# Score products of an attention layer on four quarters of the array, in a kernel on one Trainium2 core

## The chip, the cores and the metric

The kernel is one program on one core of a Trainium2 chip. The metric is the device time of one execution in microseconds, as the median of several runs. A profiled execution of the kernel before was traced instruction by instruction; all rows below come from that trace.

## The reference

Four batches of 768 positions go through windowed attention with attention sinks (8 heads of 64), and then through a channel MLP with a low-rank mixing term over positions. Everything is fp32.

```python
scores = q @ k^T / sqrt(64)                    # B=4, H=8, S=768, D=64
keep = (key < n_sink) | (0 <= query - key < window)   # n_sink=4, window=128
a = softmax(where(keep, scores, -1e9)); attn = a @ v  # (B, H, S, D)
x = attn.transpose(0, 2, 1, 3).reshape(B, S, 512)
u = x + ((x^T @ U) @ V)^T                      # U: 768x32, V: 32x768
out = u + relu(u @ w_ch1) @ w_ch2              # 512 -> 2048 -> 512
```

So each query sees at most 128 keys of its window, which ends at the query itself, and four sinks.

## The kernel before, in words

Queries are cut into six blocks of 128 per head, and heads are worked in four pairs per batch: in `qp` and `kp` the head dimension of one head lies on partitions 0 to 63 and that of the other on 64 to 127. Keys are laid out block by block, each block as four sink columns followed by its 128 keys. The scores of a query block are therefore one product with 260 neighbouring columns: the previous block's 128 keys, the four sinks, the own block's 128 keys. The first query block has no previous one and takes 132.

`scores` (the function printed below) emits, for one query block and both heads of the pair, one step on TensorE: two fp32 calls of 64 rows x 128 columns of weights (the queries) with 260 or 132 moving columns, each into its own PSUM bank. After it, for each head: VectorE copies, under the predicate `past` (key after query), the scores of the previous block over those of the own block (L734), so that 132 columns are left per query, adds the mask and takes the row's extreme (L736), and ScalarE takes the exponent with the row sum (L739). `normalise` scales the rows (L749, L757, L760), `transposes` turns three blocks (L777) and splits them into an own part and a previous part (L783, L787), and `values` multiplies with the values (L812): there the two heads lie in two column halves of the array, 128 rows x 64 columns each.

The attention of batch 0 stands at the start of the program. That of batch 1 is spread over the feed-forward products of batch 0 (L1032 to L1034 and L1054), and those of batches 2 and 3 over the products of batch 1 (L1198). Batches 1 to 3 form their feed-forward layers with fewer products over sums of quarter matrices; their weights come by DMA from DRAM (`w<-wd`, `w<-ws`) and the sums go through VectorE (L1203).

Nothing runs in the order in which it is written. Each function adds steps to a `Plan`, with a price in us, the buffers that it reads and writes, and a priority; `Plan.order` simulates all engines, tries 41 orders and keeps the one with the lowest cost by its prices. PSUM has eight banks, and a step takes whichever is free first. A step on TensorE is marked `tiled` when it runs on parts of the array, and the plan charges 0.2 us (`SWITCH`) for each change between tiled and whole and prefers to put tiled steps together. `after=self.gate` keeps the score steps of later batches from starting before a given feed-forward step.

Of the kernel before, what the change touches and what calls it, by code (L numbers as in the profile page):

```python
# [21 lines left out]
P = 128  # L22
B, H, S, D = 4, 8, 768, 64
# [65 lines left out]
def f32(ap):  # L89
    return ap.bitcast(F32)  # L90
# [185 lines left out]
class Plan:  # L276
# [7 lines left out]
    def add(self, eng, dur, fn, *args, port=False, **kw):  # L284
        return self.any({eng: (dur, fn, port)}, *args, **kw)
# [235 lines left out]
def dve(n):  # L521
    return 0.069 + n * 1.042e-3
# [6 lines left out]
def act(n):  # L529
    return 0.052 + n * 0.8333e-3  # L530
# [6 lines left out]
class Fast:  # L537
# [19 lines left out]
    def fixed(self, n, shape, dtype, name):  # L557

        ring = Ring(n, None)

        def get(view=lambda t: t):
            return ring(lambda i=len(ring.boxes) % n: view(self.place(name, i, shape, dtype)))
        get.ring, get.name = ring, name
        return get
# [146 lines left out]
    def scores(self, blocks, t0, q, k, rows):  # L711
        nc, add = self.nc, self.plan.add
        (qr, qbase), (kr, kbase) = q, k
        todo = []
        for qb in blocks:
            half, u = divmod(qb, NBLK)
            if half not in rows:
                rows[half] = self.p(), self.mn(), self.sm()
            lo = P if qb == 0 else 0
            k0 = max(qb - 1, 0) * SW + (NS if qb else 0) - kbase  # L720
            for i in range(2):
                todo.append((i, qb, u, lo, UW - lo, qb * P - qbase, k0, self.bank(), rows[half]))

        def mms():
            for i, _, _, _, wd, q0, k0, st, _ in todo:
                at = slice(i * D, (i + 1) * D)
                nc.tensor.matmul(st()[:, :wd], qr()[at, q0:q0 + P], kr()[at, k0:k0 + wd], start=True, stop=True)  # L727
        add("PE", 0.005 + sum(max(x[4], 131) for x in todo) / 1200.0, mms, r=[qr, kr] + [(x[8][0], (x[0], x[2])) for x in todo],
            w=[x[7] for x in todo], prio=t0, after=self.gate, tiled=True)
        for i, qb, u, lo, wd, _, _, st, (p, mn, sm) in todo:  # L730
            row = lambda p=p, i=i, u=u: p()[:, i, u]
            at = lambda t, i=i, u=u: t()[:, i * NBLK + u:i * NBLK + u + 1]
            if qb:
                add("DVE", dve(P), lambda st=st: nc.vector.copy_predicated(st()[:, SW:UW], self.past, st()[:, :P]),  # L734
                    w=(st,), prio=t0)
            add("DVE", dve(SW), lambda st=st, row=row, at=at, wd=wd, qb=qb, mn=mn: nc.vector.tensor_tensor_reduce(  # L736
                row(), st()[:, wd - SW:wd], self.mask[:, min(qb, 2)], -0.125, 3.0e38, ALU.add, ALU.min, at(mn)),
                r=(st,), w=((p, (i, u)), (mn, (i, u))), prio=t0)
            add("ACT", act(SW) + 0.22, lambda row=row, at=at, mn=mn, sm=sm: nc.scalar.activation(  # L739
                row(), row(), AF.Exp, bias=at(mn), scale=-1.0, accum_out=at(sm)),  # L740
                r=((mn, (i, u)),), w=((p, (i, u)), (sm, (i, u))), prio=t0)
# [50 lines left out]
    def values(self, parts, t0, v, xT):  # L792
        nc, add = self.nc, self.plan.add
        vr, kb0 = v
        todo, cost, outs = [], 0.0, []
        for half, tops in parts:
            pa = self.bank()
            kbs = range(max(half * NBLK - 1, 0), (half + 1) * NBLK)
            for n, kb in enumerate(kbs):
                lo = 2 * (kb - half * NBLK) + 1  # L800
                hi = min(lo + 2, 2 * NBLK)
                lo = max(lo, 0)
                at = max(kb - half * NBLK, 0) * P
                for i, t in enumerate(tops):
                    todo.append((pa, i, t, kb - kb0, lo * P, hi * P, at, n == 0, n == len(kbs) - 1))
            cost += 1.09 if half == 0 else 1.31
            outs.append((half, pa))

        def run():
            for pa, i, t, kb, lo, hi, at, first, last in todo:  # L810
                mv = t().rearrange("p u s j -> p (u s j)")[:, lo:hi]
                nc.tensor.matmul(pa()[i * D:(i + 1) * D, at:at + hi - lo], vr()[:, i, kb, :], mv,  # L812
                                 start=first, stop=last, skip_group_check=True)
        add("PE", cost, run, r=[vr] + [t for _, tops in parts for t in tops] + [(xT, half) for half, _ in parts],
            w=[pa for _, pa in outs], prio=t0, tiled=True)
        for half, pa in outs:
            self.copy(CH, lambda half=half: xT()[:, half * CH:(half + 1) * CH], lambda pa=pa: pa()[:, :CH], psum=True,
                      r=(pa,), w=((xT, half),), prio=t0)
# [127 lines left out]
    def sink_mix(self, half, rep, t0):  # L946

        nc, add = self.nc, self.plan.add
        vsr, by, tp, _, _, reps = self.late
        reps.append(rep)  # L950
        if half == 0:
            return

        def run():
            for blk in range(NB):
                nc.tensor.matmul(by()[:, :P], reps[blk // NBLK]()[:, blk % NBLK * P:(blk % NBLK + 1) * P],
                                 self.usf()[:, blk, :], start=blk == 0, stop=blk == NB - 1)
        add("PE", 1.32, run, r=reps + [self.usf, self.T[0]], w=(by,), prio=t0)
        part = self.pst(lambda t: f32(t)[:, :P])
        add("DVE", dve(P), lambda: nc.vector.tensor_scalar(part(), by()[:, :P], 0.25, None, ALU.mult),  # L960
            r=(by,), w=(part,), prio=t0)
        add("PE", mm(DM, 4), lambda: nc.tensor.matmul(
            tp(), part(), vsr().rearrange("p n d -> p (n d)"), start=False, stop=False),
            r=(part, vsr), w=(tp,), prio=t0)

    def warm(self, tp, t0):

        nc, bank, rows = self.nc, self.bank(), self.mask.rearrange("p a b -> p (a b)")

        def run():  # L970
            for _ in range(NWARM):
                nc.tensor.matmul(bank()[:, :3 * SW], self.ident, rows, start=True, stop=True)
        return self.plan.add("PE", mm(3 * SW, 4 * NWARM), run, r=(tp,), w=(bank,), prio=t0)
# [365 lines left out]
    def run(self):  # L1339
        tc, nc, ctx, ring, one, fixed = self.tc, self.nc, self.ctx, self.ring, self.one, self.fixed  # L1340
# [10 lines left out]
        self.ust, self.vst = fixed(1, [P, NB, P], F32R, "ust")(), fixed(1, [P, S], F32R, "vst")()  # L1351
        self.t = fixed(2, [P, DM], F32R, "t")
        self.wtiles, self.banks, self.bigs, self.accs = [], [], list(self.early), []
        bigs = Ring(NBIG, None)
        self.raw, self.end = self.share(bigs, self.bigs, lambda t: t), self.share(bigs, self.bigs, lambda t: f32(t[:, :DM]))
        self.rest = None
# [48 lines left out]
        for b in range(B):  # L1405
            prio = 70.0 + 80.0 * NCHUNK * b
# [296 lines left out]
```

## Time and profile before

| | |
|---|---|
| median of 3 runs | 680.77 us (680.75 to 680.93) |
| span of the profiled execution | 680.2 us |
| TensorE matmul busy | 665.4 us, 98% |
| VectorE busy | 532.9 us, 78% |
| ScalarE busy | 438.7 us, 64% |
| GpSimd busy | 256.1 us, 38% |

The span goes from the first to the last instruction of the profiled execution; the runs are timed apart from it. The time that lies around the span is not in the trace, and the median of the runs is 0.57 us above it. TensorE's busy time is a sum of overlapping records whose ends are modelled, so the starts of its records tell more than their durations.

### The profile page before, as it was taken

Reading aid. Unit: us, or ns where it says so; the run is one execution under the profiler, and the core shown is the slowest. Engines: PE = TensorE matmul, PEld = TensorE weight load, DVE = VectorE, ACT = ScalarE, POOL = GpSimd, SP = SyncE. Lnnn points to the kernel's source line nnn. Section 1 sums busy time; section 2 is a strip of 40 time slices with the busy share of each in tenths; the row PEclk is TensorE's granted clock in tenths of the full one; section 3 lists DMA queues with packets and bytes.
Section 4 is the critical chain, followed back from the end, with each engine's and each line's share of the span. In section 5 each row is a group of like instructions: output and inputs, shape, how many; then the busy total and the mean of one; then the engine's idle time right before and its main releaser. Section 6 shows DMA issues by size and latency. Waiting matters only on the chain.

```text
span 680.2 us, 12939 instructions
## 1 busy us (share of the span) xinstructions
PE 665.4 (98%) x3990; PEld 595.0 (87%) x3990; DVE 532.9 (78%) x1498; ACT 438.7 (64%) x1197; POOL 256.1 (38%) x310
## 2 busy tenths in 40 slices
PE   7998999999999999999999999999999999999996
PEld 5666888788889888888898799999999999999996
DVE  7989999999998888889788799655735974673483
ACT  6997698889665378885788786355436535543551
POOL 3742545547535244576473361202303311020120
PEclk9999999999999999999999999999999999999999
DMA  8649999988869699996999856899788899988883
GB/s 288 202 154 368 374 320 353 365 286 309 295 253 336 234 340 357 324 341 191 317 336 306 272 180 189 266 359 306 243 259 252 248 311 331 298 246 259 248 267 104
DMA packets 135982, 191.94 MB, mean 282 GB/s; under 512 B 10336, under 2 KB 106208, under 8 KB 135904
## 3 DMA queue, kind: packets, MB, share of 16 engines
q1 hardware_dynamic: 135616, 190.63, 83.9%
q8 instruction: 34, 0.56, 0.3%
q10 hardware_dynamic: 288, 0.39, 0.2%
q14 instruction: 44, 0.36, 0.2%
HBM read 141.70 MB, written 49.28 MB: 281 GB/s over the span
## 4 chain that ended last, share of the span: by engine, by line
PE 83%; DVE 10%; DMA 3%; ACT 2%; issue 1%; POOL 1%; SPq 0%; ACTq 0%; DVEq 0%
PE bank L1198 48%; PE bank L1054 10%; PE bank L727 5%; PE bank L812 4%; PE bank L1032 3%; PE bank L1033 3%; PE bank L1034 3%; PE bank L777 2%; DVE p L736 1%; PE bank L919 1%; DMA kp<-ud 1%; DMA w<-wd 1%; DVE w L608 1%; DVE bank L734 1%; DVE oph L783 1%
## 5 line engine op out<-in xcount | busy, mean ns | idle before, releaser
L1198 PE MATMUL bank<-w,w 128*128 128x384 f32 x678 | 133.1, 339 | 0.1
L1198 PEld LDWEIGHTS bank<-w,w 128*128 128x128 f32 x678 | 118.2, 188 | 4.4 <-issue 1.9
L739 ACT ACTIVATE p<-p,mn 128x132 f32<-128x132 f32 x192 | 75.9, 398 | 9.5 <-DVE mn L736 9.1
L1198 PE MATMUL bank<-w,spare 128*128 128x384 f32 x342 | 65.1, 335 | 0.0
L1203 DVE TENSOR_TENSOR big<-bank,big 128x384 f32<-128x384 f32 x84 | 44.7, 553 | 24.6 <-PE bank L1198 24.0
L610 POOL TENSOR_TENSOR w<-uh,w 128x384 fp32r<-128x384 f32 x22 | 23.2, 1054 | 105.7 <-ACT w L601 102.6
L1054 PE MATMUL bank<-w,hh 128*128 128x512 f32 x192 | 61.9, 404 | 0.0
L1198 PEld LDWEIGHTS bank<-w,spare 128*128 128x128 f32 x342 | 60.0, 188 | 0.0
L610 POOL TENSOR_TENSOR spare<-spare 128x128 f32<-128x128 f32 (+1 forms) x56 | 39.2, 705 | 43.0 <-DVE spare L608 17.8
L727 PE MATMUL bank<-kp,qp 64*128 64x260 f32 (+1 forms) x360 | 52.9, 392 | 1.1 <-DMA qp<-in_q_dram 0.4
L736 DVE CUSTOM_DVE_ANT_0 p<-bank,mask 128x132 f32<-128x132 f32 x192 | 50.6, 287 | 0.1
L1032 PE MATMUL bank<-ul,w 128*128 128x384 f32 x128 | 44.4, 347 | 0.9 <-POOL ul L610 0.6
L727 PEld LDWEIGHTS bank<-kp,qp 64*128 64x128 f32 x360 | 31.1, 186 | 16.0 <-issue 4.8
L734 DVE COPY_PREDICATED bank<-past,bank 128x128 f32<-128x128 int32 x160 | 41.5, 289 | 4.5 <-PE bank L727 4.3
L787 POOL TENSOR_SCALAR_AFFINE_SELECT oph<-oph 128x384 f32<-128x384 f32 x64 | 33.8, 546 | 27.3 <-ACT oph L601 27.0
L1033 PE MATMUL bank<-uh,w 128*128 128x384 f32 x128 | 43.2, 338 | 0.0
L1034 PE MATMUL bank<-uh,w 128*128 128x384 f32 x128 | 43.2, 338 | 0.0
L601 ACT CAST w<-uh 128x384 fp32r<-128x384 f32 x57 | 29.3, 515 | 20.1 <-PE bank L1198 17.9
L812 PE MATMUL bank<-oph,vp 128*64 128x256 f32 (+1 forms) x448 | 42.1, 338 | 0.0
L1198 PE MATMUL bank<-spare,w 128*128 128x384 f32 x204 | 41.9, 340 | 0.0
L812 PEld LDWEIGHTS bank<-oph,vp 128*64 128x64 f32 x448 | 28.5, 137 | 14.9 <-issue 3.9
L608 DVE TENSOR_TENSOR spare<-spare 128x128 f32<-128x128 f32 (+1 forms) x84 | 36.5, 459 | 6.2 <-DMA ws<-spare 3.1
(267 smaller groups left out, 1693.5 us busy)
## 6 DMA issues: line engine op xcount, KB each, us to landing
w<-ws SPq DMA_DIRECT2D x132, 256.0 KB, 4.3
w<-wd SPq DMA_DIRECT2D x102, 256.0 KB, 4.7
big<-in_w_dram SPq DMA_DIRECT2D x32, 512.0 KB, 5.7
ws<-spare SPq DMA_DIRECT2D x32, 512.0 KB, 5.8
spare<-ws SPq DMA_DIRECT2D x60, 256.0 KB, 4.2
wd<-w SPq DMA_DIRECT2D x32, 384.0 KB, 6.2
spare<-wd SPq DMA_DIRECT2D x42, 256.0 KB, 4.4
kp<-in_k_dram SPq DMA_DIRECT2D x12, 396.0 KB, 5.7
```

The costliest lines, as they stand in the source:

```text
L610: ways["POOL"] = (gps(n), lambda: nc.gpsimd.tensor_tensor(dst(), a(), b(), op), True)
L727: nc.tensor.matmul(st()[:, :wd], qr()[at, q0:q0 + P], kr()[at, k0:k0 + wd], start=True, stop=True)
L734: add("DVE", dve(P), lambda st=st: nc.vector.copy_predicated(st()[:, SW:UW], self.past, st()[:, :P]), w=(st,), prio=t0)
L736: add("DVE", dve(SW), lambda st=st, row=row, at=at, wd=wd, qb=qb, mn=mn: nc.vector.tensor_tensor_reduce(row(), st()[:, wd - SW:wd], self.m ...
L739: add("ACT", act(SW) + 0.22, lambda row=row, at=at, mn=mn, sm=sm: nc.scalar.activation(row(), row(), AF.Exp, bias=at(mn), scale=-1.0, accu ...
L812: nc.tensor.matmul(pa()[i * D:(i + 1) * D, at:at + hi - lo], vr()[:, i, kb, :], mv, start=first, stop=last, skip_group_check=True)
L1032: nc.tensor.matmul(ph()[:, :CH], wh, ul()[:, c, :], start=n == 0, stop=False)
L1033: nc.tensor.matmul(ph()[:, :CH], wl, uh()[:, c, :], start=False, stop=False)
L1034: nc.tensor.matmul(ph()[:, :CH], wh, uh()[:, c, :], start=False, stop=n == NC - 1)
L1054: nc.tensor.matmul(acc[k](), a()[:, sl], w()[:, :, at, m:m + P].rearrange("p d o j -> p o d j"), start=not begin and i == 0 and j == 0, st ...
L1198: nc.tensor.matmul(bank()[:, :CH], w()[:, at:at + P], u()[:, d, :] if n > 1 else u(), start=first and i == 1, stop=last and i == 3 * n, sk ...
L1203: add("DVE", dve(CH), lambda: nc.vector.tensor_tensor(x(), bank()[:, :CH], t(), ALU.add), r=(bank,) if t is x else (bank, t), w=(x,), prio ...
```

## The change

The score step calls TensorE four times instead of twice: for each head, once for the first 64 queries of the block and once for the last 64. The output of the first goes to partitions 0 to 63 of the bank and that of the second to partitions 64 to 127, so the four calls lie on four quarters of 64 rows x 64 columns. Of the 260 columns the first 64 queries take columns 0 to 195 and the last 64 take columns 64 to 259. The columns that are left out are those that the predicate never takes: the last 64 keys of the own block lie after the first 64 queries, and the first 64 keys of the previous block lie outside the window of the last 64. They keep what the bank held before. So that this is always a score, the program keeps a set of the banks that have held scores; the first use of each bank, and each first query block, takes all columns. The plan's price of the step is changed with it.

```diff
         def mms():
-            for i, _, _, _, wd, q0, k0, st, _ in todo:
+            for i, qb, _, _, wd, q0, k0, st, _ in todo:
                 at = slice(i * D, (i + 1) * D)
-                nc.tensor.matmul(st()[:, :wd], qr()[at, q0:q0 + P], kr()[at, k0:k0 + wd], start=True, stop=True)
-        add("PE", 0.005 + sum(max(x[4], 131) for x in todo) / 1200.0, mms, r=[qr, kr] + [(x[8][0], (x[0], x[2])) for x in todo],
-            w=[x[7] for x in todo], prio=t0, after=self.gate, tiled=True)
+                known = qb and st.slot in self.written
+                self.written.add(st.slot)
+                for a in (0, D):
+                    lo, n = (a, wd - D) if known else (0, wd)
+                    nc.tensor.matmul(st()[a:a + D, lo:lo + n], qr()[at, q0 + a:q0 + a + D],
+                                     kr()[at, k0 + lo:k0 + lo + n], start=True, stop=True, skip_group_check=True)
+        add("PE", 0.02 + sum(max(x[4] - (D if x[1] else 0), 131) for x in todo) / 1200.0, mms,
+            r=[qr, kr] + [(x[8][0], (x[0], x[2])) for x in todo], w=[x[7] for x in todo], prio=t0, after=self.gate, tiled=True)
...
         self.wtiles, self.banks, self.bigs, self.accs = [], [], list(self.early), []
+        self.written = set()
```

## Rows read from the trace of the kernel before

**Rows 1.** The page, busy time of each engine.

```profile
PE 665.4 (98%) x3990; PEld 595.0 (87%) x3990; DVE 532.9 (78%) x1498; ACT 438.7 (64%) x1197; POOL 256.1 (38%) x310
```

**Rows 2.** The page, the chain that ended last, by engine and by line.

```profile
PE 83%; DVE 10%; DMA 3%; ACT 2%; issue 1%; POOL 1%; SPq 0%; ACTq 0%; DVEq 0%
PE bank L1198 48%; PE bank L1054 10%; PE bank L727 5%; PE bank L812 4%; PE bank L1032 3%; PE bank L1033 3%; PE bank L1034 3%; PE bank L777 2%; DVE p L736 1%; PE bank L919 1%; DMA kp<-ud 1%; DMA w<-wd 1%; DVE w L608 1%; DVE bank L734 1%; DVE oph L783 1%
```

**Rows 3.** Stretches: PE, PEld, DVE, ACT, POOL busy (instructions), clock, DMA share, GB/s.

```profile
100.00:150.00 50.00, 50.00 (x299) 40.21 (x299) 46.74 (x141) 42.00 (x120) 26.72 (x30) 1.00 0.92 329
150.00:200.00 50.00, 49.96 (x303) 42.21 (x304) 49.05 (x131) 36.53 (x91) 26.98 (x28) 1.00 0.87 314
...
250.00:300.00 50.00, 50.00 (x346) 42.14 (x345) 40.67 (x152) 39.74 (x132) 27.41 (x37) 1.00 0.99 346
300.00:350.00 50.00, 49.42 (x312) 44.59 (x309) 43.94 (x130) 35.06 (x100) 30.40 (x40) 1.00 0.83 272
350.00:400.00 50.00, 49.53 (x342) 40.91 (x341) 41.41 (x166) 42.55 (x150) 20.56 (x29) 1.00 0.87 289
```

**Rows 4.** The chain that ended last, from 0 to 65 us, by line.

```profile
by line: DVE p L736 12.0%; DVE bank L734 9.4%; DMA big<-in_V_dram 8.1%; DVE oph L783 5.9%; DVE xT L997 5.9%; DVE nt L141 5.8%; ACT oph L601 5.4%; issue 4.7%; POOL p L760 3.0%; DVE w L608 3.0%; ACT p L739 3.0%; DVE spare L142 2.3%; DVE nr L1
```

**Rows 5.** Groups by line: score products, busy us, mean ns, idle before.

```profile
L727 PE MATMUL bank<-kp,qp 64*128 64x260 f32 (+1 forms) x360 | 52.9, 392 | 1.1 <-DMA qp<-in_q_dram 0.4 <-ACT xT L601 0.3 <-ACT oph L601 0.2
...
L727 PE MATMUL bank<-first1k,first1q 64*128 64x260 f32 (+1 forms) x12 | 2.5, 510 | 0.0
```

**Rows 6.** Pieces of that chain: start, length, what, records.

```profile
98.25 0.86 PE bank L727 x8
...
102.89 0.64 PE bank L727 x4
...
107.76 1.08 PE bank L727 x8
...
298.87 1.51 PE bank L727 x12
```

**Rows 7.** Timeline, TensorE, narrow windows around 102.8 to 103.6 us: start, length.

```profile
102.82 0.19 PEld L727 LDWEIGHTS bank<-kp,qp 64*128 64x128 f32 x2 [0.17 <-issue]
102.82 0.49 PE L727 MATMUL bank<-kp,qp 64*128 64x260 f32 x2
...
103.14 0.39 PE L727 MATMUL bank<-kp,qp 64*128 64x260 f32 x2
...
103.46 0.51 PE L1054 MATMUL bank<-w,hh 128*128 128x512 f32 x1
```

**Rows 8.** Timeline, narrow windows around 100.3 and 100.7 us: value products.

```profile
100.29 0.43 PE L812 MATMUL bank<-oph,vp 128*64 128x256 f32 x2
...
100.29 0.14 PEld L812 LDWEIGHTS bank<-oph,vp 128*64 128x64 f32 x2 [0.25 <-DVE mn L736]
...
100.55 0.39 PE L812 MATMUL bank<-oph,vp 128*64 128x256 f32 x2
```

**Rows 9.** Timeline, narrow windows from 12.3 to 12.6 us.

```profile
12.12 0.47 PE L727 MATMUL bank<-kp,qp 64*128 64x260 f32 x1
...
12.42 0.57 PE L727 MATMUL bank<-kp,qp 64*128 64x260 f32 x2
...
12.51 0.18 PEld L727 LDWEIGHTS bank<-kp,qp 64*128 64x128 f32 x1
```

**Rows 10.** Timeline, TensorE, first and last score run after 60 us.

```profile
78.20 0.93 PE L727 MATMUL bank<-kp,qp 64*128 64x132 f32 x8
...
387.97 1.58 PE L727 MATMUL bank<-kp,qp 64*128 64x260 f32 x12
```

**Rows 11.** Waits of TensorE: us in total, times, longest.

```profile
PE bank L995 <- DVE t L982: 1.5, 1, 1.5
```

**Rows 12.** Timeline, narrow windows around 101.4 and 101.5 us: value products.

```profile
101.20 0.39 PE L812 MATMUL bank<-oph,vp 128*64 128x128 f32 x4
...
101.31 0.39 PE L812 MATMUL bank<-oph,vp 128*64 128x128 f32 x4
```

## The prediction

> **What bounds the kernel now.** I began with the busy shares of the page: TensorE is busy for 665.4 of 680.2 us, VectorE for 532.9, nothing else for more than two thirds [rows 1]. A busy TensorE is not a TensorE at its peak, so the second view was the chain of work that ended last: 83% of it is TensorE, and the score line L727 is 5% of the span [rows 2]. The third was the table by stretch: from 100 us to 400 us TensorE stands idle for at most 0.6 us in each 50 [rows 3]. All 72 score steps of batches 1 to 3 lie between 78 and 390 us, inside that stretch; there a microsecond that TensorE no longer spends on scores is a microsecond that the next product starts earlier, as long as VectorE and the DMA queues keep up. They have little to spare in places: VectorE 49.05 of 50 us between 150 and 200, the DMA engines 0.99 between 250 and 300 [rows 3]. The 24 steps of batch 0 lie before 40 us, where the chain goes through VectorE, ScalarE and a DMA, and L727 is not among the leading lines [rows 4].
>
> The fourth view was the score line itself: 360 matmul records and two groups of 12 on other tiles, of which one is shown, 384 in all [rows 5]. There are 192 calls (4 batches, 8 heads, 6 query blocks), so each fp32 call leaves two records, two passes over the same columns. A step is one query block of two heads: two calls, four records.
>
> **What a score step costs now.** Pieces of the chain give it directly [rows 6]: a lone step holds TensorE for 0.64 us, two in a row 1.08, three 1.51; so a step that follows another costs 0.437, and the one that leads a run 0.64. With the first query block in the lead (132 columns) two steps take 0.86, so such a lead costs 0.425. The timeline of a lone step shows what the 0.64 is [rows 7]: the first passes of both heads start together at 102.82, the second passes together at 103.14, the next product at 103.46. The pass itself is half of a following step, 0.217 us for 260 columns (0.83 ns a column); 0.32 - 0.217 = 0.107 of the first pass is the weight load of 128 columns, which nothing hides at the head of a run, and 103.46 - 103.14 - 0.217 = about 0.10 is the change back to another shape. The two heads run side by side on the two halves, 64 rows each.
>
> **The change, part by part.** Each call becomes two, for queries 0 to 63 and 64 to 127, of 64 columns of weights and 196 moving columns (132 for the first query block, and 260 where a bank gets its first scores). A pass falls to 196 x 0.83 = 0.163 us. The total streamed rises, from 2 x 260 to 4 x 196 columns per pass, so everything hangs on whether four quarters run at once.
>
> No row shows four. Value products (L812) show two column halves of the array: both start at 100.29 and their second passes at 100.55 [rows 8], which is as much concurrency in columns as L727 has in rows. Their head costs 0.26 - 256 x 0.83 ns = 0.05 (64 columns of weights instead of 128), so the exposed load should fall from 0.107 to 0.053.
>
> What four quarters need beyond this is that later chains overtake earlier ones. At 12.12 one head runs its first pass and at 12.42 its second, while the other head's first weight load comes only at 12.51 [rows 9]: the list goes head by head, pass by pass. At 102.82 the second head's first pass therefore ran ahead of the first head's second. One blocked pass overtaken is what rows show; the fourth quarter needs three. A queue for each quarter gives it, a short look-ahead doesn't. I take four at once, since both row halves and column halves behave as independent chains, and keep two at once for the other end.
>
> The Trainium skill, "TensorE: Matmul & The Clock Gate", Part 3 (what overlaps and what doesn't), speaks against it: a weight load overlaps a matmul in flight only if its row group differs, and matmuls start strictly in program order. Here the trace disagrees with both: the second L812 load starts at 100.29 beside a matmul on the same rows [rows 8], and heads overtake [rows 7, 9]. By the first the sum would be that of the fourth rival below, by the second that of the first.
>
> With four at once, at the rows' prices:
> - A leading step: 0.64 - 0.054 (weight load) - 2 x 0.054 (passes) + 0.012 (two more chains to start; an estimate, two starts differ by under 10 ns in [rows 7]) = 0.49; saves 0.150.
> - A following step: 0.437 - 0.108 + 0.005 = 0.334; saves 0.103. The 0.005 is for two more calls, the excess of 0.437 over 2 x 0.217 taken twice.
> - A leading first query block: its passes stay at 132 columns; 0.425 - 0.054 + 0.012; saves 0.042.
>
> After 60 us the timeline has 36 runs, from the one at 78.20 to the one at 387.97 [rows 10]: 24 led by a 260-column step, 12 by a 132-column one, with 36 followers. That gives 24 x 0.150 + 12 x 0.042 + 36 x 0.103 = 3.6 + 0.5 + 3.7 = 7.8 us, of which 2.7 before 200 us (10, 4 and 10) and 5.1 after 236 (14, 8 and 26). Batch 0's 24 steps at the same mean (0.108) would be 2.6.
>
> What of this reaches the end: of the 2.7 I take two thirds, 1.8, because VectorE at 46.7 to 49.05 of 50 us [rows 3] is next to be late; of the 5.1 I take 4.3, because VectorE has 6 to 9 us of slack in each stretch there but the DMA engines none in one of three; of the 2.6 I take 1.0 (bounds 0 and 2.6), since batch 0's chain is not TensorE's [rows 4]. The up to eight full-width first uses of a bank fall into batch 0, at 0.1 us at most each, and are inside that discount. Sum 7.1 us.
>
> Edits that cost nothing by themselves: the mask, exponent and value steps are unchanged and read the same columns; columns that a quarter doesn't compute are overwritten by the predicated copy or not picked by it. The bookkeeping of banks runs while the program is built. The planner's price of a following step falls from 0.438 to 0.347 us, so the order of all engines is planned anew. No row prices another order; the longest single wait of TensorE after 50 us is 1.5 us [rows 11], and I allow that much either way.
>
> **The number.** The profiled execution spans 680.2 us, 0.57 under the 680.77 median of the runs. 680.2 - 7.1 = 673.1, plus 0.57: 673.7. If everything reached the end, 7.8 + 2.6 would give 670.4; if half did, 675.6, and with 1.5 for the new order 677. So the likeliest case has 670.5 to 677.5.
>
> **Rivals.**
> - *Only two chains at a time* (slower). Place: the issue of L727. Eight passes of 0.163 two by two are 0.653 a step. A leading step becomes 0.053 + 0.653 + 0.11 = 0.816, +0.177; a 132-column lead 0.053 + 0.44 + 0.11 = 0.603, also +0.177; a following one 0.657, +0.220. 36 x 0.177 + 36 x 0.220 = 14.3 us, and 0 to 5 for batch 0: 695 to 700. It decides from where fewer than three chains overlap (4 x 0.163 / 0.217 = 3.0). For it: no row shows more than one pass overtaken. Against: rows and columns each behave as independent.
> - *Four at once, but the time is given back*: VectorE or the weight transfers become the wait. For it VectorE and DMA in [rows 3]; against it the 0.6 us at most that TensorE now idles per 50, and VectorE's slack after 200 us. Half of the joint stages' 5.1 and nothing else: 678.3; range 677.5 to 681.
> - *Issue is the limit.* A step then has 16 records (8 loads, 8 matmuls). The closest spacing sustained in the trace is two loads and two matmuls from 101.20 to 101.31 [rows 12], 27 ns a record; 16 take 0.44 and followers gain nothing, leads 0.05 to 0.1: 678.8. Against it: those 0.11 us were what 128 columns stream, so they bound the issue from above only, and two loads and two matmuls share one start at 102.82 [rows 7].
> - *Column quarters take turns at the weights.* Four times (0.053 + 0.163) per step, 0.864: leads +0.335, followers +0.426, 27 us after 60 us, 708 or more. Rows 8 contradict it for full rows; nothing shows it for quarters.
>
> **How the numbers follow.** Chances: four at once and mostly kept 0.59 (and 0.01 below 670.5); given back 0.16, of which 0.09 is still faster by over 0.2% and 0.07 within; issue limit 0.05 (0.02 and 0.03); two chains 0.15; turns at the weights 0.03; a worse order that eats it all 0.01. About 0.2%, 1.4 us, is what a measurement of this kernel can tell from no change. Faster: 0.59 + 0.01 + 0.09 + 0.02 = 0.71; same 0.10; slower 0.19. The range leaves out the three slow cases and runs from 669.5 to 682; the predicted 673.7 is the likeliest case's.
>
> **What the profile after would show.** Right: a lone score step near 0.49 us from its first start to the next product, four first passes starting within some 20 ns, followers at 0.33, busy time of the score line down by a sixth to a fifth, TensorE's idle time per 50 us as before. Wrong by the first rival: starts in two pairs, a lone step above 0.8 us. Given back: steps at 0.49, but new idle time before L1198, L1032 or L1054, put down to VectorE or a DMA. Issue: first starts spread over 0.1 us or more. The step that I trust least is the overtaking of three blocked passes.

## The result and the profile after

The changed kernel took 673.85 us (median of four, 672.77 to 675.24), the kernel before 680.85 beside it: a ratio of 0.9888 (95% interval 0.9871 to 0.9906), 1.1% faster; the quotient of the two medians, 0.9897, lies inside the interval. The forecast was 673.7 within 669.5 to 682. The profiled execution was the longest of the four, 675.24 us, with a span of 673.5 (before: 680.2). In every execution on record that lists both, the time is 1.68 to 1.81 us above its own span. So the 0.57 us between the median and the span before is not the time around the span: by this offset the profiled execution before was itself about 1.1 us longer than its median. Both profiled executions are long ones of their kind.

The busy shares of the page, as in [rows 1]; the instruction count of TensorE rises by 384 of each kind:

```profile
PE 656.4 (97%) x4374; PEld 586.2 (87%) x4374; DVE 530.9 (79%) x1503; ACT 443.5 (66%) x1212; POOL 249.1 (37%) x300
```

What a lone score step costs now, from the timeline of TensorE in narrow windows (start, length), beside [rows 7]:

```profile
99.34 0.15 PEld L731 LDWEIGHTS bank<-kp,qp 64*64 64x64 f32 x4 [0.17 <-issue]
...
99.34 0.40 PE L731 MATMUL bank<-kp,qp 64*64 64x196 f32 x4
...
99.56 0.35 PE L731 MATMUL bank<-kp,qp 64*64 64x196 f32 x4
...
99.83 0.44 PE L1037 MATMUL bank<-ul,w 128*128 128x384 f32 x1
```

All four first passes start within some 0.02 us, all four second passes 0.22 later, and the next product at 0.49. So four chains run side by side, and the last of them overtakes three blocked passes, if the list goes head by head and pass by pass as rows 9 show it. Pieces of the chain that ended last, beside [rows 6]:

```profile
255.37 0.72 PE bank L731 x16
259.87 0.49 PE bank L731 x8
263.71 0.82 PE bank L731 x16
...
367.54 1.16 PE bank L731 x24
```

A lone step takes 0.49 us (before 0.64), each follower 0.33 to 0.34 (0.437), a first query block in the lead 0.72 - 0.33 = 0.39 (0.425).

Where the time came off, from the first and last start of two product lines, before (L1032, L1198) and after (L1037, L1203):

```profile
L1032 PE MATMUL bank<-ul,w x128: 335/337/449, 62.7 to 234.8; 128*128 128x384 f32 x128
...
L1198 PE MATMUL bank<-w,w x678: 331/335/447, 251.1 to 674.8; 128*128 128x384 f32 x170
```

```profile
L1037 PE MATMUL bank<-ul,w x128: 335/337/448, 62.2 to 232.9; 128*128 128x384 f32 x128
...
L1203 PE MATMUL bank<-w,w x678: 331/334/446, 246.4 to 668.1; 128*128 128x384 f32 x170
```

The feed-forward products start 0.4 us earlier (62.66 and 62.24 with one more digit), the stage of batch 0's products ends 1.9 earlier, the last product starts 6.7 earlier. From the first of these products to the last it is 612.1 us before and 605.9 after.

Against that stands what TensorE waits for in the changed kernel between 60 and 400 us (us in total, times, longest):

```profile
PE bank L948 <- POOL xhl L610: 1.2, 1, 1.2
PE bank L1203 <- DMA w<-ws: 1.1, 1, 1.1
PE bank L907 <- DVE xT L910: 0.9, 2, 0.7
PE bank L1037 <- POOL ul L610: 0.7, 1, 0.7
PE bank L1037 <- DVE xT L910: 0.6, 1, 0.6
```

GpSimd, VectorE and weight transfers are named there, none of them more than twice at one place. Two of these waits stand in the kernel before as well, and shorter:

```profile
PE bank L1032 <- POOL ul L610: 0.6, 1, 0.6
...
PE bank L902 <- DVE xT L905: 0.2, 1, 0.2
```

In all, TensorE idles for 5.5 of these 340 us, against 2.2 before.

### The profile page after: what moved, and what is told of

The parts are those of the page before. It is cut to its first block, busy times and chain, and to the rows that moved or that the text cites. A ratio compares the mean times of both kernels' runs of the same rounds, so it can differ in the third digit from the quotient of the medians.

```text
span 673.5 us, 13737 instructions
## 1 busy us (share of the span) xinstructions
PE 656.4 (97%) x4374; PEld 586.2 (87%) x4374; DVE 530.9 (79%) x1503; ACT 443.5 (66%) x1212; POOL 249.1 (37%) x300
## 4 chain that ended last, share of the span: by engine, by line
PE 63%; DVE 5%; DMA 2%; issue 1%; POOL 1%; ACT 1%; SPq 0%; POOLq 0%
PE bank L1203 50%; PE bank L817 3%; PE bank L731 2%; PE bank L1059 2%; PE bank L782 1%; DMA ws<-spare 1%; DVE spare L608 1%; PE bank L924 1%; DMA w<-wd 1%; DVE xT L608 1%; PE bank L1037 1%; PE bank L948 1%; PE bank L1039 1%; PE bank L1038 1%; PE bank L947 1%
## 5 line engine op out<-in xcount | busy, mean ns | idle before, releaser
L1203 PE MATMUL bank<-w,w 128*128 128x384 f32 x678 | 131.4, 338 | 0.4 <-DMA w<-wd 0.3
L1203 PEld LDWEIGHTS bank<-w,w 128*128 128x128 f32 x678 | 118.2, 188 | 3.3 <-issue 2.4
L610 POOL TENSOR_TENSOR w<-uh,w 128x384 fp32r<-128x384 f32 x25 | 26.6, 1064 | 104.3 <-PE bank L1203 58.9
L1203 PE MATMUL bank<-w,spare 128*128 128x384 f32 x342 | 64.8, 335 | 0.0
L610 POOL TENSOR_TENSOR spare<-spare 128x128 f32<-128x128 f32 (+1 forms) x57 | 40.8, 725 | 60.8 <-DMA ws<-spare 16.7
L1203 PEld LDWEIGHTS bank<-w,spare 128*128 128x128 f32 x342 | 60.0, 188 | 0.0
L792 POOL TENSOR_SCALAR_AFFINE_SELECT oph<-oph 128x384 f32<-128x384 f32 x64 | 36.9, 592 | 31.2 <-ACT oph L601 27.7
L1037 PE MATMUL bank<-ul,w 128*128 128x384 f32 x128 | 44.6, 349 | 1.4 <-POOL ul L610 0.7
L1203 PE MATMUL bank<-spare,w 128*128 128x384 f32 x204 | 41.9, 340 | 0.2 <-DVE uh L1208 0.2
L1059 PEld LDWEIGHTS bank<-w,hh 128*128 128x128 f32 x192 | 34.6, 188 | 7.9 <-issue 2.3
L731 PE MATMUL bank<-kp,qp 64*64 64x196 f32 (+1 forms) x720 | 40.5, 334 | 0.5 <-DMA qp<-in_q_dram 0.4
L601 ACT CAST w<-ul 128x384 fp32r<-128x384 f32 x55 | 28.2, 515 | 17.8 <-PE bank L1203 17.1
```

What stands on the lines that cost most here:

```text
L601: return self.plan.any({"ACT": (act(n) + (0.0 if psum else 0.07), lambda: nc.scalar.copy(dst(), src()), False), "DVE": (dve(n) if psum els ...
L610: ways["POOL"] = (gps(n), lambda: nc.gpsimd.tensor_tensor(dst(), a(), b(), op), True)
L731: nc.tensor.matmul(st()[a:a + D, lo:lo + n], qr()[at, q0 + a:q0 + a + D], kr()[at, k0 + lo:k0 + lo + n], start=True, stop=True, skip_group ...
L1037: nc.tensor.matmul(ph()[:, :CH], wh, ul()[:, c, :], start=n == 0, stop=False)
L1059: nc.tensor.matmul(acc[k](), a()[:, sl], w()[:, :, at, m:m + P].rearrange("p d o j -> p o d j"), start=not begin and i == 0 and j == 0, st ...
L1203: nc.tensor.matmul(bank()[:, :CH], w()[:, at:at + P], u()[:, d, :] if n > 1 else u(), start=first and i == 1, stop=last and i == 3 * n, sk ...
```

## The experiments

All runs below are compared with the kernel before on their own chip, where its median was 682.1 to 682.5 us; so ratios are what compares across runs.

**Shorter steps or another order?** The new price led the planner to another order of all engines. Two runs take the two apart: the new calls in the old order, and the old calls in the new order.

```diff
 # e1: the changed kernel with the price of before
-        add("PE", 0.02 + sum(max(x[4] - (D if x[1] else 0), 131) for x in todo) / 1200.0, mms,
+        add("PE", 0.005 + sum(max(x[4], 131) for x in todo) / 1200.0, mms,
 # e2: the kernel before with the price of the changed one
-        add("PE", 0.005 + sum(max(x[4], 131) for x in todo) / 1200.0, mms,
+        add("PE", 0.02 + sum(max(x[4] - (D if x[1] else 0), 131) for x in todo) / 1200.0, mms,
```

> Four quarter calls as in the changed kernel, but the step keeps the price of before, so the planner puts every engine's work in the order of the kernel before. Theory (the time comes from shorter score steps: 0.49 us alone, 0.33 following, instead of 0.64 and 0.44): steps are as short as in the changed kernel and the median is 673 to 675 us. Rival (the time comes from the new order that the new price led to): 679 to 681 us.

> The two half-array calls of before, with only the price of the changed kernel, so the order of the changed kernel with the old steps. Theory (shorter steps): 680 to 682 us, the steps at 0.64 and 0.44 us. Rival (new order): 673 to 676 us.

New calls in the old order: 676.9 us, ratio 0.9927 (0.9905 to 0.9949). Old calls in the new order: 681.94, ratio 0.9982 (0.9963 to 1.0). So the shorter steps carry the gain: 0.7% in the old order, and in the new one 0.9982 - 0.9888 = 0.9%. The order alone is worth 0.2%, at the edge of what can be measured. In microseconds the first run lies between the theory's range and its rival's, 1.9 above the one and 2.1 below the other; as a ratio it is nearer to the theory, whose upper end of 675 us is 0.991 of 680.85, while the rival's lower end is 0.997.

The first and the last start of the same two product lines, e1 and then e2, show where the time comes off:

```profile
L1037 PE MATMUL bank<-ul,w x128: 335/337/448, 63.3 to 234.2; 128*128 128x384 f32 x128
...
L1203 PE MATMUL bank<-w,w x678: 331/334/446, 250.3 to 669.0; 128*128 128x384 f32 x170
```

```profile
L1032 PE MATMUL bank<-ul,w x128: 335/337/448, 62.8 to 236.3; 128*128 128x384 f32 x128
...
L1198 PE MATMUL bank<-w,w x678: 331/334/446, 250.1 to 674.9; 128*128 128x384 f32 x170
```

From the first product to the last it is 605.7 us with the new calls in the old order and 612.1 with the old calls in the new one. The changed kernel has 605.9 and the kernel before 612.1. So behind the first product the two orders can't be told apart in these executions, and the shorter steps are worth 6.4 us in the old one and 6.2 in the new one. What else separates e1 from the changed kernel lies ahead of that product.

The score line and all of TensorE from 60 to 400 us (window, its length, then busy us and instructions; the line alone first, then all lines), for the pair with the new order. Old calls:

```profile
60.00:400.00 340.00, 39.28 (x288) 23.14 (x288) 1.00 0.88 307
...
60.00:400.00 340.00, 336.15 (x2057) 285.01 (x2055) 299.82 (x928) 256.68 (x750) 169.98 (x201) 1.00 0.88 307
```

The changed kernel, whose calls alone differ from that run's:

```profile
60.00:400.00 340.00, 31.38 (x576) 17.57 (x576) 1.00 0.90 313
...
60.00:400.00 340.00, 334.54 (x2381) 284.90 (x2380) 303.07 (x939) 261.38 (x767) 173.16 (x205) 1.00 0.90 313
```

The line gets 7.9 us shorter, idle time grows by 1.6 (340 - 334.54 against 340 - 336.15), and the spans are 680.5 and 673.5. In the old order the same subtraction gives 41.11 - 32.90 = 8.2 for the line and 1.2 more idle time, with spans 680.2 and 674.4. The line before, and in e1:

```profile
60.00:400.00 340.00, 41.11 (x288) 24.10 (x288) 1.00 0.89 311
```

```profile
60.00:400.00 340.00, 32.90 (x576) 18.09 (x576) 1.00 0.90 313
```

**What batch 0 gives.** Its calls stay on halves; batches 1 to 3 go on quarters.

```diff
+        todo, gated = [], bool(self.gate)
...
+                if not gated:
+                    nc.tensor.matmul(st()[:, :wd], qr()[at, q0:q0 + P], kr()[at, k0:k0 + wd], start=True, stop=True)
+                    self.written.add(st.slot)
+                    continue
```

> Quarters for batches 1 to 3 alone; batch 0 keeps the two half-array calls, price and order as in the changed kernel. Theory (batch 0 is bound by VectorE and ScalarE; the first feed-forward product started only 0.4 us earlier in the changed kernel): 673.5 to 674.5 us, and the half-clock stretch at 16.6 to 20 us may be gone. Rival (batch 0 gave its third, 1 us, or more): 674.8 to 676 us.

675.04 us, ratio 0.9901 (0.9872 to 0.9931), span 672.4. That is within the interval of the changed kernel. In microseconds it lies in the range of the rival, by its ratio (674.1 of 680.85) in that of the theory, and its interval spans 2 us to either side, so the time decides nothing. In the profile the first feed-forward product starts at 61.7, no later than with quarters. Quarters in batch 0 bring nothing that can be seen. Stretches 10 to 15 and 15 to 20 us say one thing more (the clock is the third number from the end). The changed kernel:

```profile
10.00:15.00 5.00, 3.44 (x40) 1.74 (x34) 5.00 (x31) 5.00 (x26) 1.29 (x2) 1.00 1.08 364
15.00:20.00 5.00, 4.86 (x35) 3.00 (x36) 4.97 (x33) 4.67 (x21) 2.72 (x6) 0.66 0.50 159
```

With halves in batch 0:

```profile
10.00:15.00 5.00, 3.79 (x25) 2.40 (x23) 5.00 (x29) 5.00 (x26) 1.21 (x2) 1.00 1.08 365
15.00:20.00 5.00, 4.91 (x33) 3.32 (x34) 4.96 (x33) 4.64 (x21) 2.81 (x6) 1.00 0.52 167
```

VectorE and ScalarE are busy for all of the first stretch; TensorE waits for them, and with shorter steps it waits longer. In the changed kernel the granted clock is then 0.66 on the mean of the next stretch, part of it at the lower of its two levels, 1.2 GHz; with halves it stays at 2.4 in this execution. But halves do not ensure that: e2 has the old calls throughout and also falls.

```profile
10.00:15.00 5.00, 3.78 (x25) 2.32 (x23) 5.00 (x29) 5.00 (x25) 1.15 (x2) 1.00 1.08 364
15.00:20.00 5.00, 4.90 (x22) 3.25 (x22) 4.84 (x33) 4.64 (x21) 2.87 (x6) 0.69 0.41 127
```

The clock also differs between executions of one kernel: the mean over the span lies between 0.991 and 1.0 in the 41 executions of the kernel before that list it. So the fall is not shown to come from the quarters. What batch 0's quarters save may be lost there, or was never on the path.

**Columns or weight loads?** Four quarters, each with all 260 columns.

```diff
-                    lo, n = (a, wd - D) if known else (0, wd)
+                    lo, n = (0, wd)
```

> Four quarters at once, but each takes all 260 columns (same output, more columns streamed), price and order of the changed kernel. Theory (the gain is the 64 columns less per quarter, and a little the shorter weight load): a lone step at 0.60, a following one at 0.44 us, median 678.5 to 681 us. Rival (it is the weight loads and the fourfold start that pay, not the columns): 674 to 676 us. If four wide streams get in each other's way, a following step would be well above 0.44 us.

680.1 us, ratio 0.9971 (0.9958 to 0.9984). Its pieces of the chain:

```profile
258.07 0.82 PE bank L731 x16
262.68 0.60 PE bank L731 x8
266.62 1.04 PE bank L731 x16
```

A lone step 0.60, a follower 1.04 - 0.60 = 0.44, as expected: four wide streams don't disturb each other here, the shorter weight load is worth 0.04 of a lead, and the rest of the gain is the 64 columns less.

**How far does overtaking go?** Groups of 32 queries on 64 rows x 32 columns, eight calls a step with 164 columns each.

```diff
-                for a in (0, D):
-                    lo, n = (a, wd - D) if known else (0, wd)
-                    nc.tensor.matmul(st()[a:a + D, lo:lo + n], qr()[at, q0 + a:q0 + a + D],
+                for a in range(0, P, 32):
+                    lo, n = (a, wd - 96) if known else (0, wd)
+                    nc.tensor.matmul(st()[a:a + 32, lo:lo + n], qr()[at, q0 + a:q0 + a + 32],
```

> Each head's step is cut into four groups of 32 queries (64 rows x 32 columns of the array, 164 key columns each), eight calls a step; price and order of the changed kernel. If as many chains run at once as there are parts (seven blocked passes overtaken), a pass is 0.136 us, a following step 0.28 to 0.30, a lone one 0.43 to 0.45, and the median 670.5 to 672.5 us. If overtaking ends at the three of the changed kernel, a following step is about 0.55 us and the median 684 to 690 us. If the issue of 32 records a step is the limit, in between: 673 to 676 us.

```profile
99.53 0.44 PE bank L731 x16
101.75 0.72 PE bank L731 x32
```

A lone step 0.44, a follower 0.28: eight chains at once, seven blocked passes overtaken. But the median is 673.68, ratio 0.9863 (0.983 to 0.9896), which can't be told from the changed kernel's, though the line from 60 to 400 us is another 3 us shorter (28.43). Nor can it be told from what I expected: by its ratio it is 671.5 of 680.85 us, inside 670.5 to 672.5. The one trace shows nothing kept: TensorE's idle time there grew from 5.5 to 6.7, and from the first to the last product it is 668.9 - 62.6 = 606.3 us, against 605.9.

**Is VectorE what takes the rest back?** Both kernels without the predicated copies (L734); in the changed one a bank counts as written only from its first full use.

```diff
-                add("DVE", dve(P), lambda st=st: nc.vector.copy_predicated(st()[:, SW:UW], self.past, st()[:, :P]),
+                add("DVE", dve(P), lambda st=st: None,
```

> The kernel before without the predicated copies (46 us of VectorE work left out, with it the scores of the previous block), planned in the same order. It is the reference for the next run. If VectorE holds TensorE up in the kernel before, 676 to 679 us; if not, 680 to 681.

> The changed kernel without the predicated copies, planned in the same order (each bank's first full-width use is also kept at all columns). Theory (VectorE takes back part of the shorter steps: 9.9 us saved after 60 us, 6.3 kept): the distance to the kernel before without copies is 8 to 10 us. Rival (other waits, DMA or the order, take it back): the distance stays at 6 to 7.5 us.

The kernel before without copies: 682.18 us, ratio 0.9993 (0.9973 to 1.0013), with VectorE's busy time from 60 to 400 us down from 304.71 to 281.56. The changed one: 674.87, ratio 0.9894 (0.9862 to 0.9926), VectorE down from 303.07 to 286.02. The distance is 1.0% (7.3 us of the medians), as with copies. So the medians give the theory no support; but with the two intervals put together (an estimate) the distance lies between some 4.7 and 9.9 us, so they don't exclude its 8 to 10. All of TensorE from 60 to 400 us, before and changed, both without copies:

```profile
60.00:400.00 340.00, 337.32 (x2064) 286.62 (x2063) 281.56 (x813) 255.65 (x749) 177.13 (x209) 1.00 0.90 310
```

```profile
60.00:400.00 340.00, 336.52 (x2395) 287.52 (x2394) 286.02 (x823) 261.10 (x767) 173.87 (x206) 1.00 0.90 313
```

The changed kernel's idle time is 3.5 us without copies, against 5.5 with them, and from the first to the last product the distance is 612.7 - 604.4 = 8.3 us. In the stage of batch 0's products (the first to the last start of L1037) nothing moves, 170.6 us without copies and 170.7 with them. So VectorE's work does not hold that stage up; in the later stages it may cost a microsecond or two, which these runs leave open.

**A floor for the step.** Quarters of 64 columns, the same order; the scores of all other columns are left out, and a bank counts as written as in the run before.

```diff
-                    lo, n = (a, wd - D) if known else (0, wd)
+                    lo, n = (a, D) if known else (0, wd)
```

> Four quarters with 64 columns each (most of the scores left out), price and order of the changed kernel, to see the floor of a step with 16 records. If streaming and loading set it, a following step takes 0.11 to 0.15 us and a lone one about 0.28. If 27 ns a record were the issue limit, 0.43 us.

```profile
296.50 0.39 PE bank L732 x16
302.67 0.28 PE bank L732 x8
```

A lone step 0.28, a follower 0.11, so issue keeps up with 16 records in 0.11 us, 7 ns a record; it is no limit here. The line is down to 19.40 us from 60 to 400, 12 us less than in the changed kernel. Yet the one execution has a span of 672.4, only 1.1 less. Part of that may be clock, whose mean is 0.989, against 0.996 in the changed kernel's profile. TensorE idles for 9.3 us there (340 - 330.67, against 5.5), and in one stretch the clock falls too, behind one in which TensorE was busy for 3.53 of 5 us:

```profile
350.00:355.00 5.00, 3.53 (x46) 2.29 (x45) 3.52 (x16) 2.83 (x12) 1.74 (x2) 1.00 0.84 277
355.00:360.00 5.00, 4.57 (x20) 4.47 (x21) 3.88 (x14) 3.77 (x16) 2.67 (x3) 0.67 1.00 341
```

From the first to the last product it is 667.0 - 62.4 = 604.6 us, 1.3 less than in the changed kernel. So in an order made for steps of 0.49 and 0.33 us, nearly all that the much shorter steps save is given back in this execution.

**Is it the order that holds the rest?** Four runs on one chip: the changed kernel again, the eighths and the 64-column quarters with prices as measured, and the changed kernel with another constant.

```diff
 # e9: eighths
+        add("PE", 0.005 + sum(x[4] - (96 if x[1] else 0) for x in todo) / 1200.0, mms,
 # e10: the changed kernel
+        add("PE", 0.005 + sum(max(x[4] - (D if x[1] else 0), 131) for x in todo) / 1200.0, mms,
 # e11: quarters of 64 columns
+        add("PE", 0.01 + sum(D if x[1] else x[4] for x in todo) / 1200.0, mms,
```

> The changed kernel once more, on the chip of the next three runs, so that they can be compared with it. About 0.989 of the kernel before, as the first time.

> The groups of 32 queries of the earlier run, with the price that the steps were measured at there (0.278 us following), so that the planner orders for them. Theory (what holds the time up after the change is the fixed order of the engines' queues, which was made for longer steps): 1 to 3 us under the changed kernel. Rival (something other than TensorE's share of the scores sets the time by now, whatever the order): within 1 us of the changed kernel.

> The changed kernel with 0.005 in place of 0.02 in the price of the step, the 0.332 us that a following step was measured at. The calls are the same and the order of all engines is another one: this shows what an order alone is worth. Theory of a real gain by shorter steps: within 1.5 us of the changed kernel, on either side. If orders differ by 3 us or more, the share of the change that I put down to the order is no finding.

> The quarters of 64 columns (most scores left out) with their own price, 0.117 us following. Against the changed kernel 15 us of TensorE time are gone, as in the run without the price, which was only 1 us shorter. Theory (fixed order): with an order made for it 5 us or more come off, 661 to 668 us. Rival (another resource is the limit of the stages with scores by now): 669 to 673 us, with TensorE waiting for VectorE, ScalarE or weight transfers there.

| kernel | median us | ratio (95% interval) |
|---|---|---|
| e8, the changed kernel again | 674.51 | 0.9876 (0.985 to 0.9901) |
| e9, eighths, own price | 678.64 | 0.9929 (0.9907 to 0.9951) |
| e10, changed kernel, 0.005 | 677.06 | 0.991 (0.9881 to 0.994) |
| e11, 64 columns, own price | 668.75 | 0.9801 (0.9773 to 0.9829) |

The 64-column quarters gain 5.8 us on the changed kernel once the order is made for them; without it their one execution gained about 1. In microseconds 668.75 lies between the two ranges, 0.75 above the theory's and 0.25 below the rival's. The same calls in the order of the changed kernel (e7) and in their own (e11) decide it:

```profile
L1038 PE MATMUL bank<-ul,w x128: 335/338/445, 62.4 to 232.7; 128*128 128x384 f32 x128
...
L1204 PE MATMUL bank<-w,w x678: 331/334/446, 245.5 to 667.0; 128*128 128x384 f32 x170
```

```profile
L1038 PE MATMUL bank<-ul,w x128: 332/336/448, 66.2 to 237.3; 128*128 128x384 f32 x128
...
L1204 PE MATMUL bank<-w,w x678: 331/334/446, 247.8 to 661.4; 128*128 128x384 f32 x170
```

From the first to the last product it is 604.6 us in the one order and 595.2 in the other, with 450 matmul records ahead of the first in both. So behind the first product the fixed order held 9.4 us of the 12; the new order starts that product 3.8 us later. The eighths lost 4 us by being planned for, where I expected 1 to 3 less: the planner's best order by its own prices is not the best on the chip. Its TensorE from 60 to 75 us:

```profile
60.00:65.00 5.00, 5.00 (x28) 4.43 (x27) 5.00 (x13) 3.93 (x10) 2.01 (x2) 1.00 1.04 411
65.00:70.00 5.00, 3.06 (x13) 2.27 (x12) 4.28 (x11) 3.27 (x6) 1.28 (x1) 0.87 1.04 410
70.00:75.00 5.00, 5.00 (x20) 4.07 (x19) 4.16 (x9) 2.50 (x4) 1.30 (x1) 0.79 0.97 311
```

TensorE idles for 1.9 us in the middle stretch and the clock falls in it and behind it. And the same calls as in the changed kernel, in the order of another constant (e10), took 2.6 us longer, more than the 1.5 that I expected, with overlapping intervals. Much of this goes with the granted clock: the six spans of e10 are 673.5 to 674.3 in the three executions at a mean clock of 0.994 to 1.0, and 676.3 to 678.2 in the three at 0.989 and 0.990, while e8's four are 671.7 to 674.3 at 0.994 and 0.995. No run that computes the whole output beats the changed kernel by more than the intervals; the eighths in its order are level with it.

## Why the prediction was right

**The step's price** was right in every part. Four quarters run at once; a lead was put at 0.49, a follower at 0.334, a 132-column lead at 0.425 - 0.042 = 0.383, and the rows show 0.49, 0.33 to 0.34 and 0.39. The sum after 60 us was put at 7.8; with the order kept, the line got 7.9 and 8.2 us shorter. The split into weight load (0.054 of a lead) and passes is shown by e4, whose leads lost only the load. The choice that carried it, that a later chain overtakes more blocked passes than rows 9 show, was right with room to spare: eight chains ran at once.

**What reaches the end** came out near the sum, 6.7 of the span against 7.1, but not by the steps that I gave. Batch 0 was put at 1.0; the first feed-forward product came 0.4 us earlier, and with halves in batch 0 it came no later. Behind that product 1.8 + 4.3 = 6.1 were put, and 6.2 (new order) and 6.4 (old order) came. The discount on batch 1 was put down to VectorE; but that stage takes 170.6 us without the copies and 170.7 with them, so the reason was wrong. Of the 2.7 the stage kept 2.8 in the new order (173.5 to 170.7) and 1.2 in the old one (172.1 to 170.9), so it is luck that the 1.8 lies between them. One sign failed: TensorE's idle time was to stay as it was, and it rose from 2.2 to 5.5 us between 60 and 400. What takes part of the saving back is waits at single places, on GpSimd, VectorE and weight transfers in turn, in queues whose order is fixed. That the order can hold a saving back is shown by e7 and e11, 604.6 and 595.2 us with the same calls; for the changed kernel itself it is argued. Which wait matters most was not settled.

**The hit within 0.2 us owes something to luck.** The allowance was 1.5 us for a new order. The same calls stand at 0.9927 of the kernel before in the old order, 0.991 in a third, 0.9888 and 0.9876 in the one that was timed: of 680.8 us that is 675.8, 674.7, 673.2 and 672.4. All lie in the likeliest case's 670.5 to 677.5. How much of the differences is order is not shown: behind the first product the old order and the timed one give the same time, and the clock differs between executions.

**The rivals.** Two chains at a time: refuted by the timeline after (four starts at 99.34). Issue as the limit: refuted by e7 (0.11 us for a step of 16 records). Turns at the weights: refuted by the same timeline, four loads at 99.34. Given back: not at this size, but it is what happened to most of a further saving in e7; in e5 the interval leaves it open. The rule of the Trainium skill, "TensorE: Matmul & The Clock Gate", Part 3, that a load overlaps a matmul only where the row group differs and that matmuls start in program order, does not hold for these fp32 passes: loads and passes of two column quarters on the same rows start within some 0.02 us of each other, ahead of passes listed before them.

## What to carry to other kernels

Where a mask makes some columns of a product useless to part of its rows, cutting it into parts of the array that each leave out their useless columns can pay even if the total streamed rises: here from 2 x 260 to 4 x 196 columns a pass, with a follower at 0.33 us in place of 0.437. Four parts with all 260 columns left the follower at 0.44 (e4). Such a step was priced well as its longest chain of passes, plus the weight load of one part, plus the change of shape. In a kernel whose queues are ordered ahead of time, price the change with the order kept, and time it in more than one order: here one edit stood 5.2 to 7.9 us below the kernel before of its chip in three orders. Look at the clock of each execution before putting such a spread down to the order. When one more saving on the busiest engine moves nothing, look at its idle time in the same stretch before looking for a busier engine.

## What was not expected of the hardware

Eight chains of two fp32 passes on 64 x 32 parts start within one step of 0.44 us, and 32 records issue in a follower of 0.28 us. The granted clock fell to its lower level in or behind stretches in which TensorE was busy for 3.06 (e9), 3.44 (the changed kernel), 3.53 (e7) and 3.78 (e2) of 5 us, but not in e3 behind 3.79, nor at the start of the kernel before, where 10 to 15 us has 3.08 of 5 busy and the next stretch is at 1.00:

```profile
10.00:15.00 5.00, 3.08 (x21) 1.85 (x18) 5.00 (x33) 5.00 (x26) 1.69 (x3) 1.00 1.08 364
15.00:20.00 5.00, 5.00 (x38) 3.23 (x37) 4.65 (x31) 4.86 (x25) 4.11 (x8) 1.00 0.51 171
```

The fall comes with old calls (e2) and new ones alike, and the changed kernel's other profiled execution (e8) has 0.50 between 15 and 20 us, where the first has 0.66. Whether a faster step on TensorE costs clock is therefore not shown, and what decides the fall was not settled.
